# A new written order for the first three head pairs and the steady loop of an attention and soft-MoE kernel, with 66-column values and three more resident weight tiles

## The chip, the core and the metric

The kernel runs on one core of a Trainium2 chip. The metric is the device time of one execution in microseconds (us); one run of the changed kernel is compared with runs of the kernel before on the same chip. The engines are TensorE (PE in the rows; PEld is its weight load), VectorE (DVE), ScalarE (ACT), GpSimd (POOL) and SyncE (SP), which issues most DMAs.

## The reference

Attention over 8 batches of 8 heads, 576 positions of 64 numbers, and a soft mixture of experts on its output, all in float32:

```python
q_rot, k_rot = rotate(q), rotate(k)
scores = (1 / sqrt(D)) * q_rot @ k_rot.T
attn = exp(scores - scores.max(-1)); attn /= attn.sum(-1) + 1e-09
x = (attn @ v) -> (4608, 512)              # 8 heads side by side
logits = x @ phi                           # 32 slots, 4 for each of 8 experts
d = softmax of logits over all 4608 rows;  slot_input = d.T @ x
slot_out[e] = relu(slot_input[e] @ w1[e]) @ w2[e]      # w1 512x1024, w2 1024x512
out = softmax of logits over the 32 slots @ slot_out
```

## The kernel before

The 64 heads are worked as 32 pairs of heads; four pairs make a batch. For each pair p the work is cut into named steps, each a small function that issues its instructions on its engines:

- load0, load1 (line 136, SP): rotary inputs of q and k into one of two x buffers, 576 KB each; load_v (161): the values with a column of ones.
- spin0, spin1 (141, GpSimd): four multiplications each with cosines and sines; "rotations" below. join (146, VectorE) adds the halves. high0, high1 (150, ScalarE) cast to float16 into an operand buffer; low (155, VectorE) takes the remainder, after which the x buffer is free for pair p+2.
- m00 to m31 and m_rem (171, 181): a coarse score product on PE and a maximum over it on VectorE; m_min, m_turn, m_half (193 to 206) turn the maxima into a row, m_rows (208) sends that row by two small DMAs into the tile peak, from SP (for pair 0 from ScalarE's queue).
- t0 to t7 (214): one score part each, eight float16 matmuls, the last two of them with the peaks; ScalarE follows with the exponential. t8 (229) is the remainder part of the 64 last positions.
- av0 to av4 (249): the products with the values. One of av0 to av3 is 18 units; a float32 unit is two matmul instructions, so 36 stand in the trace. Units run two side by side on halves of the array (four in av4). The ones column gives the row sums.
- o_out (278, ScalarE) copies the result out of PSUM, recip (289, VectorE) inverts the sums, norm (295, GpSimd) multiplies into the x tile xn of the batch, natural and natural_out (321, 327) transpose it on PE.
- Once per batch: logits (336) and bs0 to bs6, which run the statistics, the slot product (382: transposes, then matmuls that read xn) and the combine weights.

The score, maximum, transpose and remainder steps share three PSUM buffers of two banks (168); each product waits until the reader of the buffer three before it is done. The value products have one buffer.

The order of all this is written by hand as numbers: WHEN gives each step a due time for a pair (line 51; one pair is 4 units), EARLY (62) replaces it for named steps of the first pairs, and lines 609 to 618 sort the steps by these and issue them. Within one engine instructions run in the order issued; the times themselves are not enforced. Ahead of that, pair 0 is loaded and rotated in halves on VectorE (588 to 602).

Weights are 64 tiles of 512 KB (32 of w1, 32 of w2). N_W tiles of the pool wp are loaded along the pairs, one per pair from pair 2 on (556); N_CST and N_WA tiles follow when the x buffers are done (481), one and N_WE when the operand buffers are done (492), N_WL when the attention's tiles are done (501). The other tiles are loaded in the last stage (714 to 717 and 808), where the slots run through the experts (725 to 759), and the result is combined and sent out in 18 DMAs of 512 KB (772).

Of the kernel before, what the change touches and what calls it, by code (L numbers as in the profile page):

```python
# [19 lines left out]
DM = H * D  # L20
# [7 lines left out]
N_W = 24  # L28
N_WA = 5
N_WB = 2  # L30
N_WE = 3
# [17 lines left out]
CUT = 320  # L49
WIDE = True  # L50
WHEN = {
    "load0": -13.475, "spin0": -13.456, "load1": -13.036, "spin1": -12.384, "join": -11.941, "high0": -11.78,
    "high1": -11.78, "low": -8.673, "m21": -8.574, "m20": -8.467, "m30": -7.842, "m10": -7.783, "m11": -7.689,
    "m_rem": -6.685, "m00": -5.636, "m01": -5.354, "m31": -4.383, "m_min": -2.621, "weights": -1.922, "m_turn":
# [3 lines left out]
    5.267, "recip": 7.247, "norm": 8.094, "natural": 10.815, "natural_out": 10.826, "logits_late": 10.828,  # L58
    "logits_out_late": 11.426, "logits": 13.466, "logits_out": 14.024, "bs0": 14.124, "bs1": 15.06, "bs2":
    17.43, "bs3": 19.118, "bs4": 19.678, "bs5": 20.487, "bs6": 22.6,  # L60
}
EARLY = {
# [3 lines left out]
    -16.25, ("m_rem", 0): -16, ("m_min", 0): -15.75, ("m_turn", 0): -15.5, ("m_half", 0): -15.25, ("m_rows", 0):  # L66
    -15, ("heat", 0): -14.75, ("join0", 1): -14.5, ("high0", 1): -14.25, ("m00", 1): -14, ("m01", 1): -13.75,
    ("m10", 1): -13.5, ("m11", 1): -13.25, ("low", 1): -13, ("load0", 3): -12.75, ("load1", 3): -12.5, ("spin0",
    2): -12.25, ("spin1", 2): -12,
}  # L70
QL, QH, KH, KL = range(4)
TERMS = ((KH, QH), (KH, QL), (KL, QH), (None, None))


# [818 lines left out]
```

## Time and profile before

| | us |
|---|---|
| median of 3 runs | 553.19 |
| lowest and highest | 552.36, 553.56 |
| the profiled execution's own time | 553.2 |
| its span from the first to the last instruction | 551.3 |

A row of the page's slices cuts the span into 40 equal parts of 13.8 us; a digit is the busy share in tenths, and PEclk is the granted clock of TensorE in tenths of full speed. The chain of waits follows the work that ended last back to the start; each of its rows is a stretch of that chain. A group of lines gives count, busy time, mean duration and idle time before.

### The profile page before, as it was taken

What the parts mean: (1) busy time and instruction counts of PE and PEld (TensorE: products, weight loads), DVE (VectorE), ACT (ScalarE), POOL (GpSimd) and SP (SyncE); (2) the same over time, 40 slices, a digit from 0 to 9 for tenths busy, and PEclk for the clock granted to TensorE, in tenths of its full rate; (3) what the DMA queues carried; (4) which work ended last, traced back from release to release, by engine and by line L of the source; (5) the groups of instructions that cost most, each with busy time, mean ns of one, the idle gap of its engine ahead of it and who ended that gap; (6) DMA issues with size and microseconds to landing.
All of it is one profiled execution on the core that took longest, in us unless ns stands there. A gap on an engine that the chain in (4) does not pass through costs nothing.

```text
span 551.3 us, 23417 instructions
## 1 busy us (share of the span) xinstructions
PE 510.1 (93%) x10420; PEld 376.9 (68%) x10420; DVE 366.0 (66%) x610; ACT 313.2 (57%) x688; POOL 283.3 (51%) x356
## 2 busy tenths in 40 slices
PE   3658999999999999999999999999999999899982
PEld 2226777778778777877777778677877777644551
DVE  5777877886787778777877787678777611232352
ACT  2124666666666656675666666666666566254441
POOL 2954666666576557655965686558662211210000
PEclk9657999999999999999999999999999999999997
DMA  7242644444444444444444444443330532549998
GB/s 243 92 172 66 210 157 167 156 151 152 151 152 150 152 152 150 152 151 152 151 152 150 150 153 153 150 150 113 113 113 27 217 104 65 204 144 410 409 416 340
DMA packets 28484, 93.87 MB, mean 170 GB/s; under 512 B 4064, under 2 KB 5856, under 8 KB 28384
## 3 DMA queue, kind: packets, MB, share of 16 engines
q1 hardware_dynamic: 28370, 92.37, 47.0%
q8 instruction: 82, 1.34, 1.0%
q14 instruction: 18, 0.15, 0.1%
q10 hardware_dynamic: 14, 0.00, 0.0%
HBM read 82.85 MB, written 9.44 MB: 167 GB/s over the span
## 4 chain that ended last, share of the span: by engine, by line
PE 84%; DVE 5%; DMA 5%; POOL 1%; ACT 1%; issue 1%; SPq 0%; ACTq 0%; DVEq 0%; POOLq 0%
PE o_ps L255 31%; PE s_ps L226 23%; PE s_ps L177 7%; PE s_ps L325 4%; PE s_ps L240 3%; PE s_ps L729 3%; PE s_ps L342 2%; DVE nm L179 2%; DMA w_exp<-in_w 2%; PE s_ps L185 2%; DMA x_in<-in_qk 2%; PE s_ps L201 1%; PE s_ps L396 1%; POOL x_in L144 1%; PE s_ps L753 1%; DMA out<-w_exp 1%
## 5 line engine op out<-in xcount | busy, mean ns | idle before, releaser
L144 POOL TENSOR_TENSOR x_in<-x_in,cs_sb 128x288 f32<-128x288 f32 x248 | 198.1, 833 | 103.0 <-DMA x_in<-in_qk 90.0
L179 DVE TENSOR_REDUCE nm<-s_ps 128x2 f32<-128x576 f32 x256 | 184.6, 754 | 76.9 <-PE s_ps L177 75.2
L227 ACT ACTIVATE a_t<-s_ps 128x576 f32<-128x576 f32 x256 | 153.5, 653 | 129.6 <-PE s_ps L226 129.4
L255 PE MATMUL o_ps<-v_in,a_t 128*64 128x65 f32 x4608 | 163.0, 225 | 0.7 <-ACT a_t L227 0.7
L255 PEld LDWEIGHTS o_ps<-v_in,a_t 128*64 128x64 f32 x4608 | 145.5, 138 | 26.5 <-issue 21.1
L226 PE MATMUL s_ps<-hl 64*128 64x288 f16 x1536 | 134.0, 286 | 2.9 <-DVE nm L179 2.5
L226 PEld LDWEIGHTS <-hl 64*128 64x128 f16 x1536 | 71.2, 95 | 32.3 <-issue 15.1
L226 PE MATMUL s_ps<-peak,lift 64*128 64x288 f16 x512 | 74.4, 286 | 1.1 <-DMA peak<-mr 1.1
L177 PE MATMUL s_ps<-hl 64*128 64x288 f16 x512 | 65.8, 293 | 9.4 <-DVE nm L179 6.9
L301 POOL TENSOR_TENSOR xn<-o_sb,rr 128x512 f32<-128x512 f32 x31 | 48.3, 1558 | 34.8 <-DVE rr L293 33.4
L153 ACT CAST hl<-x_in 128x576 f16<-128x576 f32 (+1 forms) x66 | 40.9, 678 | 26.8 <-DVE x_in L148 25.0
L148 DVE TENSOR_TENSOR x_in<-x_in 128x1152 f32<-128x1152 f32 (+2 forms) x36 | 46.5, 1291 | 3.3 <-POOL x_in L144 3.2
L157 DVE TENSOR_TENSOR hl<-x_in,hl 128x1152 f16<-128x1152 f32 x32 | 44.9, 1402 | 0.5 <-ACT hl L153 0.5
L177 PEld LDWEIGHTS <-hl 64*128 64x128 f16 x512 | 25.4, 95 | 25.8 <-issue 10.5
L416 POOL TENSOR_TENSOR ln<-ln,cm 128x160 f32<-128x160 f32 x7 | 9.4, 1348 | 46.7 <-DVE cm L415 46.7
L226 PEld LDWEIGHTS <-lift 64*128 64x128 f16 x512 | 25.7, 95 | 7.7 <-issue 1.3
L187 DVE TENSOR_REDUCE nm<-s_ps 128x2 f32<-128x576 f32 x32 | 24.3, 759 | 5.2 <-PE s_ps L185 5.0
L255 PEld LDWEIGHTS o_ps<-v_in,a_tr 64*64 64x64 f32 x1152 | 21.5, 134 | 7.5 <-issue 7.4
L255 PE MATMUL o_ps<-v_in,a_tr 64*64 64x65 f32 x1152 | 26.0, 224 | 0.0
L325 PE MATMUL s_ps<-id_sb,xn 128*128 128x128 f32 x160 | 23.7, 279 | 1.7 <-DVE xn L316 1.7
L240 PE MATMUL s_ps<-hl 64*64 64x320 f16 (+1 forms) x384 | 22.9, 291 | 0.6 <-issue 0.6
L325 PEld LDWEIGHTS s_ps<-id_sb,xn 128*128 128x128 f32 x160 | 16.9, 140 | 9.4 <-issue 8.6
(175 smaller groups left out, 490.6 us busy)
## 6 DMA issues: line engine op xcount, KB each, us to landing
x_in<-in_qk SPq DMA_DIRECT2D x62, 576.0 KB
w_exp<-in_w SPq DMA_DIRECT2D x63, 512.0 KB
v_in<-in_v SPq DMA_DIRECT2D x32, 325.0 KB
out<-w_exp SPq DMA_DIRECT2D x18, 512.0 KB
x_in<-in_qk SPq DMA_DIRECT2D x4, 288.0 KB
cs_sb<-in_cs SPq DMA_DIRECT2D x2, 288.0 KB
wk<-in_w SPq DMA_DIRECT2D x1, 512.0 KB
peak<-mr SPq DMA_DIRECT2D x31, 2.0 KB
```

The source lines that it names most:

```text
L144: eng.tensor_tensor(out=x[:, :, c], in0=x[:, :, c], in1=cs_sb[:, :, c], op=ALU.mult)
L148: nc.vector.tensor_tensor(out=x[:, t, 0, c], in0=x[:, t, 0, c], in1=x[:, t, 1, c], op=ALU.add)
L153: nc.scalar.copy(out=halves[p][:, 1 + t, c], in_=loaded[p][:, t, 0, c])
L157: nc.vector.tensor_tensor(out=hl[:, 0:4:3], in0=x[:, :, 0], in1=hl[:, 1:3], op=ALU.subtract)
L177: nc.tensor.matmul(s[c, h, 0:HC], lhsT=hl[rows[h], QH, P * j + c.start:P * j + c.stop], rhs=hl[rows[h], KH, half[n]], start=True, stop=True)
L179: nc.vector.tensor_reduce(out=nms[p][:, n, j:8:4], in_=s[:, :, 0:HC], axis=AX.X, op=ALU.max, negate=True)
L226: nc.tensor.matmul(s[c, h, 0:HC], lhsT=lhs, rhs=rhs, start=(x == 0), stop=(x == 3))
L227: nc.scalar.activation(out=ats[p, b][:, :, half[n]], in_=s[:, :, 0:HC], func=AF.Exp, scale=SCALE)
L240: nc.tensor.matmul(s[rows[h ^ n], n, 0:w] if n else s[rows[h], 0, 512 - w:512], lhsT=lhs, rhs=rhs, start=(x == 0), stop=(x == 3))
L255: nc.tensor.matmul(o[rows[c], h, 65 * u:65 * u + 65], lhsT=lhs, rhs=v, start=(i == 0 and u == first), stop=stop)
L301: eng.tensor_tensor(out=xn[:, :, 0:4], in0=t[:, :, 0:4, 0:64], in1=rr[:, :, 0:4].unsqueeze(3).broadcast_to([P, 2, 4, 64]), op=ALU.mult)
L325: nc.tensor.transpose(t[:, P * j:P * j + P], xns[b][:, j, pp * P:pp * P + P], id_sb)
```

## The change

The order numbers are new, both for the steady loop and, for every step of pairs 0, 1 and 2, for the start. N_W goes from 24 to 28 and N_WE from 3 to 2. There is one xn tile instead of two and there are three operand buffers instead of four. The values have two columns of ones, so that a unit of the value product has 66 columns and its rows lie 66 numbers apart in PSUM and in the copies. The listing of EARLY is cut.

```diff
--- before.py
+++ after.py
@@ -25,10 +25,10 @@
 CM = 4096.0
 BIG = 3.0e38
 HC = S // 2
-N_W = 24
+N_W = 28
 N_WA = 5
 N_WB = 2
-N_WE = 3
+N_WE = 2
 N_WL = 1
 N_X = 5
 N_O = 2
@@ -47,26 +47,47 @@
 N_A = 3
 N_AR = 1
 CUT = 320
+VW = 66
+N_HL = 3
+N_XN = 1
 WIDE = True
 WHEN = {
-    "load0": -13.475, "spin0": -13.456, "load1": -13.036, "spin1": -12.384, "join": -11.941, "high0": -11.78,
-    "high1": -11.78, "low": -8.673, "m21": -8.574, "m20": -8.467, "m30": -7.842, "m10": -7.783, "m11": -7.689,
-    "m_rem": -6.685, "m00": -5.636, "m01": -5.354, "m31": -4.383, "m_min": -2.621, "weights": -1.922, "m_turn":
-    -1.57, "m_half": -1.488, "m_rows": -0.172, "t0": 0, "t5": 0.097, "t1": 0.15, "t6": 0.268, "trickle0": 0.55,
-    "t8": 1.396, "trickle1": 1.55, "t4": 2.038, "load_v": 2.313, "av0": 2.403, "trickle2": 2.55, "t7": 2.782,
-    "t3": 2.79, "av2": 3.319, "trickle3": 3.55, "av3": 3.997, "t2": 4.028, "av1": 4.176, "av4": 4.327, "o_out":
-    5.267, "recip": 7.247, "norm": 8.094, "natural": 10.815, "natural_out": 10.826, "logits_late": 10.828,
-    "logits_out_late": 11.426, "logits": 13.466, "logits_out": 14.024, "bs0": 14.124, "bs1": 15.06, "bs2":
-    17.43, "bs3": 19.118, "bs4": 19.678, "bs5": 20.487, "bs6": 22.6,
+    "load0": -9.5660, "load1": -9.2923, "spin0": -9.2495, "spin1": -9.1951, "join": -8.6148, "high1": -8.5102,
+    "high0": -7.7527, "low": -5.7077, "m01": -4.7860, "m21": -4.6203, "m10": -4.0010, "m11": -3.9990, "m31":
+    -3.8399, "m30": -3.6599, "m00": -3.6538, "m20": -3.6507, "m_rem": -3.2198, "m_min": -1.9015, "m_turn":
+    -1.2741, "m_half": -1.2400, "weights": -1.0103, "load_v": -0.9825, "m_rows": -0.3931, "t0": 0.0000, "t7":
+    0.1234, "t1": 0.3483, "trickle0": 0.5500, "trickle1": 1.5500, "t8": 1.6955, "trickle2": 2.5500, "av0":
+    2.7124, "t2": 3.2150, "t6": 3.2160, "t5": 3.3121, "t3": 3.3621, "t4": 3.3631, "trickle3": 3.5500, "av3":
+    3.8550, "av1": 4.0015, "av2": 4.3433, "av4": 4.3578, "o_out": 5.2000, "recip": 11.3621, "norm": 12.5850,
+    "natural": 14.5258, "natural_out": 14.6310, "logits_late": 14.6330, "logits": 14.9987, "logits_out":
+    15.0778, "logits_out_late": 15.2310, "bs0": 15.3754, "bs1": 16.0452, "bs2": 16.3082, "bs3": 18.6955, "bs4":
+    18.8882, "bs5": 20.0488, "bs6": 23.2242,
 }
 EARLY = {
...
+    ("low", 0): -10015.2, ("m21", 0): -10012.6, ("m10", 0): -10010.6, ("m_rem", 0): -19.7239, ("m01", 0):
+    -19.7229, ("m30", 0): -19.2249, ("spin0", 1): -17.3334, ("m00", 0): -11.1708, ("m20", 0): -9.6275, ("m11",
+    0): -9.3361, ("m31", 0): -8.3516, ("spin1", 1): -7.6792, ("m_min", 0): -7.4843, ("join0", 1): -7.4833,
+    ("load0", 2): -3.7748, ("m_turn", 0): -3.6049, ("heat", 0): -3.3212, ("m_half", 0): -3.2702, ("join1", 1):
+    -2.2295, ("high1", 1): -2.0637, ("high0", 1): -1.575, ("load1", 2): -1.2863, ("low", 1): -1.0997, ("m11",
+    1): -1.088, ("m_rows", 0): -0.7274, ("m01", 1): -0.5995, ("t8", 0): -0.2355, ("t0", 0): -0.1016, ("m21", 1):
+    0.2211, ("t1", 0): 0.329, ("m10", 1): 0.3399, ("m30", 1): 0.6838, ("t2", 0): 0.6899, ("spin0", 2): 0.6977,
+    ("spin1", 2): 0.8581, ("join", 2): 0.8727, ("load_v", 1): 0.9223, ("t4", 0): 0.9233, ("t3", 0): 1.0977,
+    ("m00", 1): 1.1147, ("high1", 2): 1.1367, ("m_rem", 1): 1.1429, ("high0", 2): 1.1587, ("av0", 0): 1.4005,
+    ("m20", 1): 1.9295, ("t7", 0): 1.9305, ("m31", 1): 2.1643, ("m_min", 1): 2.1821, ("av1", 0): 2.237,
+    ("m_turn", 1): 2.257, ("m_half", 1): 2.2755, ("low", 2): 2.4753, ("t6", 0): 3.0355, ("m11", 2): 3.0722,
+    ("t5", 0): 3.1918, ("m31", 2): 3.2158, ("m_rows", 1): 3.2339, ("m01", 2): 3.2793, ("av3", 0): 3.3978,
+    ("m30", 2): 3.4347, ("t1", 1): 3.4357, ("m20", 2): 3.7798, ("av2", 0): 3.922, ("m00", 2): 4.1088, ("t0", 1):
...
 }
 QL, QH, KH, KL = range(4)
 TERMS = ((KH, QH), (KH, QL), (KL, QH), (None, None))
@@ -87,7 +108,7 @@
     trans = ctx.enter_context(ExitStack())
     att = trans.enter_context(tc.tile_pool(name="att", bufs=1))
     early = ctx.enter_context(ExitStack())
-    stk = early.enter_context(tc.tile_pool(name="stk", bufs=4))
+    stk = early.enter_context(tc.tile_pool(name="stk", bufs=N_HL))
     right = ctx.enter_context(ExitStack())
     io = right.enter_context(tc.tile_pool(name="io", bufs=1, side="right"))
     banks = ctx.enter_context(ExitStack())
@@ -159,7 +180,7 @@
     vts = {}
 
     def load_v(p):
-        vts[p] = att.tile([P, 2 * NB + 2, 65], F32, name="v_in", bufs=2)
+        vts[p] = att.tile([P, 2 * NB + 2, VW], F32, name="v_in", bufs=2)
         nc.sync.dma_start(out=vts[p], in_=v[p])
 
     nms = {}
@@ -252,7 +273,7 @@
         o, vt, at = os_[p], vts[p], ats.pop((p, i))
 
         def unit(lhs, c, h, u, v, stop=False):
-            nc.tensor.matmul(o[rows[c], h, 65 * u:65 * u + 65], lhsT=lhs, rhs=v, start=(i == 0 and u == first), stop=stop)
+            nc.tensor.matmul(o[rows[c], h, VW * u:VW * u + VW], lhsT=lhs, rhs=v, start=(i == 0 and u == first), stop=stop)
 
         if i < NB:
             first = 0
@@ -270,17 +291,17 @@
 
     xts = {}
     xns = {}
-    xn_sb = [xp.tile([P, 5, DM], F32, name=f"xn{i}") for i in range(2)]
+    xn_sb = [xp.tile([P, 5, DM], F32, name=f"xn{i}") for i in range(N_XN)]
     for t in xn_sb:
         nc.gpsimd.memset(t[64:P, 4], 0.0)
     osb = {}
 
     def o_out(p):
-        osb[p] = t = att.tile([P, 2, 5, 65], F32, name="o_sb", bufs=N_O)
+        osb[p] = t = att.tile([P, 2, 5, VW], F32, name="o_sb", bufs=N_O)
         o = os_.pop(p)
-        nc.scalar.copy(out=t.rearrange("p h u x -> p h (u x)")[:, :, 0:260], in_=o[:, :, 0:260])
+        nc.scalar.copy(out=t.rearrange("p h u x -> p h (u x)")[:, :, 0:4 * VW], in_=o[:, :, 0:4 * VW])
         for h in range(2):
-            nc.scalar.copy(out=t[0:64, h, 4], in_=o[rows[h], h, 260:325])
+            nc.scalar.copy(out=t[0:64, h, 4], in_=o[rows[h], h, 4 * VW:5 * VW])
 
     rrs = [const.tile([P, 2, 5], F32, name=f"rr{i}") for i in range(2)]
     for t in rrs:
@@ -295,7 +316,7 @@
     def norm(p, eng):
         b, pp = divmod(p, NP)
         if pp == 0:
-            xns[b] = xn_sb[b % 2]
+            xns[b] = xn_sb[b % N_XN]
         xn = xns[b][:, :, pp * P:(pp + 1) * P].rearrange("p j (h x) -> p h j x", h=2)
         t, rr = osb.pop(p), rrs[p % 2]
         eng.tensor_tensor(out=xn[:, :, 0:4], in0=t[:, :, 0:4, 0:64],
@@ -304,9 +325,9 @@
                           in1=rr[0:64, :, 4].unsqueeze(2).broadcast_to([64, 2, 64]), op=ALU.mult)
 
     def norm_last(p):
-        o = os_.pop(p)[:, :, 0:325].rearrange("p h (u x) -> p h u x", x=65)
+        o = os_.pop(p)[:, :, 0:5 * VW].rearrange("p h (u x) -> p h u x", x=VW)
         rr, pp = rrs[p % 2], p % NP
-        odd = small.tile([P, 2, 65], F32, name="odd", bufs=1)
+        odd = small.tile([P, 2, VW], F32, name="odd", bufs=1)
         for h in range(2):
             nc.scalar.copy(out=odd[0:64, h], in_=o[rows[h], h, 4])
         nc.vector.tensor_scalar_add(out=rr[:, :, 0:4], in0=o[:, :, 0:4, 64], scalar1=1e-9)
@@ -856,7 +877,7 @@
     vm = vr[:, :, :128 * NB].reshape(NPAIR, 2, NB, 128, D).transpose(0, 3, 2, 1, 4).reshape(NPAIR, 128, 2 * NB, D)
     ve = np.stack([vr[:, :, 128 * NB:], vr[:, ::-1, 128 * NB:]], axis=3).reshape(NPAIR, 128, 2, D)
     vl = np.concatenate([vm, ve], axis=2)
-    vl = np.concatenate([vl, np.ones_like(vl[..., :1])], axis=-1)
+    vl = np.concatenate([vl, np.ones_like(vl[..., :VW - D])], axis=-1)
 
     w1 = moe_w1.reshape(2, 4, 2, 2, 128, 2, 512).transpose(0, 5, 2, 1, 4, 3, 6).reshape(4 * E, 128, 1024)
     w2 = moe_w2.reshape(2, 4, 2, 4, 128, 2, 256).transpose(5, 0, 2, 1, 4, 3, 6).reshape(4 * E, 128, 1024)
```

What the numbers make of one period of the steady loop on PE, with the pair relative to p in brackets (none stands for p), without the pieces that come once per batch:

```text
before: t0 t2(-1) t5 t1 m30(+2) | av1(-1) | m10(+2) t6 m11(+2) | av4(-1) m_rem(+2) t8 | t4 m00(+2) |
        av0 m_turn(+1) | m01(+2) t7 t3 | natural(-2) | av2 | m21(+3) m20(+3) m31(+2) | av3
after:  m10(+1) t0 m11(+1) | av1(-1) | t7 m31(+1) m30(+1) | av2(-1) | m00(+1) t1 m20(+1) |
        av4(-1) m_rem(+1) t8 | natural(-3) | av0 m_turn(+1) | m01(+2) t2 t6 t5 t3 t4 m21(+2) | av3
```

In the same way the start, after the prologue, the first column the pair:

```text
before: PE 0: m00 m01 m10 m11 m20 m21 m30 m31 m_rem m_turn heat, 1: m00 m01 m10 m11 m21 m20 m30 m_rem,
        2: m21 m20, 1: m31, 0: t0 t5 t1, 2: m30 m10, 0: t6, 2: m11 m_rem, 0: t8 t4, 2: m00, 0: av0, ...
        0: av2 av3 av1 av4; VectorE has join1(1) after m21(0), ScalarE m_rows(0) ahead of high0(1)
after:  PE 0: m21 m10 m_rem m01 m30 m00 m20 m11 m31 m_turn heat, 1: m11 m01, 0: t8 t0, 1: m21, 0: t1,
        1: m10 m30, 0: t2 t4 t3, 1: m00 m_rem, 0: av0, 1: m20, 0: t7, 1: m31, 0: av1, 1: m_turn, 0: t6,
        2: m11, 0: t5, 2: m31 m01, 0: av3, 2: m30, 1: t1, 2: m20, 0: av2, 2: m00, 1: t0, 2: m10, 0: av4;
        VectorE has join0(1) join1(1) after m_min(0), ScalarE high1(1) high0(1) ahead of m_rows(0)
```

## Rows read from the trace of the kernel before

**Rows 1.** The page: its first line, and of its part 2 PE, clock and traffic in 40 slices.
```profile
span 551.3 us, 23417 instructions
...
PE   3658999999999999999999999999999999899982
...
PEclk9657999999999999999999999999999999999997
...
GB/s 243 92 172 66 210 157 167 156 151 152 151 152 150 152 152 150 152 151 152 151 152 150 150 153 153 150 150 113 113 113 27 217 104 65 204 144 410 409 416 340
```

**Rows 2.** Stage windows, start to 45 us: stretch, length, busy time (instructions) by engine.
```profile
15.00:30.00 15.00, 8.37 (x45) 3.94 (x43) 11.23 (x16) 1.61 (x3) 11.21 (x14) 0.61 0.22 74
30.00:45.00 15.00, 7.85 (x66) 4.85 (x67) 11.70 (x14) 4.99 (x8) 11.66 (x13) 0.50 0.46 158
```

**Rows 3.** Chain of waits, 12 to 49 us: start, duration (us), what.
```profile
13.30 3.21 DVE nm L179 x5
...
20.55 0.18 DVE min L195
...
28.11 1.36 DVE hl L157
...
29.48 3.73 DMA x_in<-in_qk
...
33.34 5.82 POOL x_in L144 x7
```

**Rows 4.** Timeline of PE, 0 to 70 us: start, duration (us), instructions merged.
```profile
46.87 2.17 PE L255 MATMUL o_ps<-v_in,a_t 128*64 128x65 f32 x36
...
58.12 0.23 PE L255 MATMUL o_ps<-v_in,a_tr 64*64 64x65 f32 x2
```

**Rows 5.** Timelines of VectorE and ScalarE, 0 to 70 us.
```profile
17.20 1.10 DVE L148 TENSOR_TENSOR x_in<-x_in 128x576 f32<-128x576 f32 x1
...
18.34 0.67 ACT L153 CAST hl<-x_in 128x576 f16<-128x576 f32 x1 [6.43 <-DVE x_in L148]
...
21.74 1.13 ACTq L210 DMA_DIRECT2D peak<-mr  x1
22.89 0.52 ACTq L211 DMA_DIRECT2D peak<-mr  x1
```

**Rows 6.** Chain of waits on the plateau, 200 to 226 us.
```profile
212.39 0.47 PE s_ps L177 x6
212.86 1.20 PE o_ps L255 x36
214.06 2.07 PE s_ps L226 x32
...
217.73 0.49 PE s_ps L226 x8
...
218.34 0.68 PE o_ps L255 x34
```

**Rows 7.** Chain of waits at the end, 440 us to the end.
```profile
451.13 1.46 PE s_ps L342 x64
...
456.62 2.25 PE o_ps L255 x72
...
517.58 10.37 DMA w_exp<-in_w
```

**Rows 8.** Groups by line and form, whole span: count, busy us, mean ns, idle before.
```profile
L144 POOL TENSOR_TENSOR x_in<-x_in,cs_sb 128x288 f32<-128x288 f32 x248 | 198.1, 833 | 103.0 <-DMA x_in<-in_qk 90.0 <-DMA id_sb<-in_ident 9.5 <-DVE x_in L148 3.0
L179 DVE TENSOR_REDUCE nm<-s_ps 128x2 f32<-128x576 f32 x256 | 184.6, 754 | 76.9 <-PE s_ps L177 75.2
L255 PE MATMUL o_ps<-v_in,a_t 128*64 128x65 f32 x4608 | 163.0, 225 | 0.7 <-ACT a_t L227 0.7
...
L301 POOL TENSOR_TENSOR xn<-o_sb,rr 128x512 f32<-128x512 f32 x31 | 48.3, 1558 | 34.8 <-DVE rr L293 33.4 <-ACT xt L334 0.8 <-ACT a_t L227 0.6
...
L255 PE MATMUL o_ps<-v_in,a_tr 64*64 64x65 f32 x1152 | 26.0, 224 | 0.0
```

More of the change, by code (lines that the diff above doesn't have):

```diff
@@ L49 @@
 CUT = 320
+VW = 66
+N_HL = 3
+N_XN = 1
 WIDE = True
 WHEN = {
-    "load0": -13.475, "spin0": -13.456, "load1": -13.036, "spin1": -12.384, "join": -11.941, "high0": -11.78,
-    "high1": -11.78, "low": -8.673, "m21": -8.574, "m20": -8.467, "m30": -7.842, "m10": -7.783, "m11": -7.689,
-    "m_rem": -6.685, "m00": -5.636, "m01": -5.354, "m31": -4.383, "m_min": -2.621, "weights": -1.922, "m_turn":
[3 rows of a table removed]
-    5.267, "recip": 7.247, "norm": 8.094, "natural": 10.815, "natural_out": 10.826, "logits_late": 10.828,
-    "logits_out_late": 11.426, "logits": 13.466, "logits_out": 14.024, "bs0": 14.124, "bs1": 15.06, "bs2":
-    17.43, "bs3": 19.118, "bs4": 19.678, "bs5": 20.487, "bs6": 22.6,
[3 rows of a table added]
+    -1.2741, "m_half": -1.2400, "weights": -1.0103, "load_v": -0.9825, "m_rows": -0.3931, "t0": 0.0000, "t7":
[3 rows of a table added]
+    "natural": 14.5258, "natural_out": 14.6310, "logits_late": 14.6330, "logits": 14.9987, "logits_out":
+    15.0778, "logits_out_late": 15.2310, "bs0": 15.3754, "bs1": 16.0452, "bs2": 16.3082, "bs3": 18.6955, "bs4":
+    18.8882, "bs5": 20.0488, "bs6": 23.2242,
 }
 EARLY = {
[3 rows of a table removed]
[L66 to L69, printed above, removed]
[3 rows of a table added]
+    ("load0", 2): -3.7748, ("m_turn", 0): -3.6049, ("heat", 0): -3.3212, ("m_half", 0): -3.2702, ("join1", 1):
[6 rows of a table added]
+    ("m_turn", 1): 2.257, ("m_half", 1): 2.2755, ("low", 2): 2.4753, ("t6", 0): 3.0355, ("m11", 2): 3.0722,
[4 rows of a table added]
+    ("av0", 1): 6.9412, ("m_min", 2): 7.0216, ("m_turn", 2): 7.1357, ("m_half", 2): 7.2769, ("m_rows", 2):
[5 rows of a table added]
+    ("recip", 1): 13.5847, ("natural", 0): 13.7449, ("natural_out", 0): 14.1101, ("recip", 2): 15.215, ("norm",
+    2): 15.6059, ("norm", 1): 16.8154, ("natural", 1): 17.9791, ("natural_out", 1): 18.0735, ("natural", 2):
+    21.6965, ("natural_out", 2): 22.3948, ("small_loads", 0): 23.215,
 }
```

10 rows, old and new, of the table EARLY are left out of this document.

## The prediction

> **What bounds the kernel now.** I read the page first, then the stage windows, then the chain of waits, and last the timelines of single engines where the chain points. The page says that TensorE is busy nearly everywhere, but it also shows three stages with different limits: the first three slices, where PE stands at 3 to 6 tenths and its clock is granted at half for much of the time; a long plateau at 9; and the last slices, where PE is still "busy" but the memory traffic jumps from about 150 to over 400 GB/s [rows 1]. The windows confirm the first: in 15 to 45 us PE does 45 and 66 instructions per 15 us, while VectorE and GpSimd are busy for nearly 12 of the 15 [rows 2].
>
> The start is an order problem. The chain runs low(0), the row maxima of pair 0, the minimum, then the maxima of pair 1, low(1) at 28.11, the load of pair 3 at 29.48 (its buffer is free only after low(1)), and eight rotations of pair 3 on GpSimd from 33.34 [rows 3]. Only after that does the first value product of pair 0 start, at 46.87, and at half clock: 2.17 us where it later takes 1.20 [rows 4, 6]. Yet the operands of pair 0 were complete at 13.3 and its row maxima at 20.7 [rows 3]; nothing but the written order holds its scores back. On the plateau the chain is PE alone. Its blocks have fixed prices: a score part 0.49, a maximum part 0.12, a value product 1.20, and a group of three maxima between two value products 0.47, not 0.36 [rows 6]: entering this kind of matmul after another costs 0.11. Two value products side by side take 2.25, so the second costs 1.05 and entering costs 0.15 [rows 7]. At the end PE waits 10.37 us for a weight tile [rows 7], with the DMA at about 410 GB/s through the last four slices [rows 1]: this stage is paid by the byte.
>
> **Part by part. The start.** Up to low(0) at 13.30 nothing changes. Then nine maximum reductions follow without the half join of pair 1 (1.10, rows 5) between them, so the minimum ends at about 20.73 - 1.0 = 19.7 [rows 3]. The two half joins of pair 1 follow: 21.9. ScalarE has high1, high0 of pair 1 (0.67 each) and then issues the row peaks of pair 0 (1.13 + 0.52): 23.2 and 24.9 [rows 5]. This is a move for the worse: before, the peaks were issued at 21.74, ahead of the second cast. ScalarE has nothing else queued behind it but the first exponential, which needs the peaks anyway. How long the 2 KB take to land no row tells; between nothing and the 3.73 us of a 576 KB load [rows 3] I take 2, so the last term of the first score part runs at 27. From there PE has, up to the end of av4(0), in the new order: ten score parts (4.9), thirteen maxima (1.6), four value products (4.8), av4 (0.68), remainder and transpose (about 0.5), and six entries (0.7): 13.2 us at full clock [rows 6, 7]. VectorE over the same stretch, from low(1) at 24.6: sixteen reductions at some 0.70, two joins of 1.4, one low of 1.36, 15.6 us [rows 8, 3]; it ends level with PE, so the two will wait for each other now and then. PE comes out of a nearly idle stretch and, as in 28 to 48 us before, starts at half clock: I add 2.5 for that and the waits together. av4(0) ends at 43; before it ended at 58.35 [rows 4]. At that point the old order had done more: two score parts and seven or eight maxima ahead, 1.9 us of PE time. Gain 58.35 - 43 - 1.9 = **13.4, taken as 13**. Bounds: 10 if half clock holds through most of the 13.2 us, 15 if neither clock nor waits cost anything. The loads and rotations cover it: pair 3 is loaded when low(1) ends (24.6 instead of 29.48), its eight rotations end some 10.5 us later as before (33.34 + 8 x 0.83 - 29.48), at 35, and its join stands behind the maxima of pair 2, at 37. The value load of pair 1 now stands ahead of the peaks of pair 1 on SP and waits for nothing; the small loads go far behind, where their first user is still later.
>
> **The steady order.** Old: five groups of score and maximum parts per pair, four value products (none adjacent), one remainder group, one transpose group. New: four such groups, the rest the same. One entry less, -0.11 per pair [rows 6]. The batch pieces move the other way: the two transposes of the batch statistics and the slot product now split score groups, two entries per four pairs, +0.05 per pair. Five score parts now stand in a row where there were four; four cost 2.07 where 4 x 0.49 + 0.11 would be 2.07 [rows 6], so the three banks hide ScalarE; a fifth may add 0.05. Over some 28 pairs: **-2 taken**, between -4 (old irregular stalls go as well) and +5 (the tighter order adds 0.2 per pair).
>
> **One x buffer, three operand buffers.** The single x buffer makes the first normalisation of a batch wait for the slot product of the batch before. Behind it on GpSimd stand eight rotations (6.7) and behind those the join; per pair GpSimd has 6.7 + 2.1 = 8.8 us of work in 12.6 [rows 8], and the rotations are wanted only at the end of the period, by my count 0.6 us after they end in that period and 5 us after they end in the other three. Cost nothing; if that cover is gone, VectorE's join and ScalarE's cast come late and each microsecond of it costs up to 7 in all, once per batch. The operand buffer of pair p is asked for by the cast of pair p+3 right behind the exponential of the last score part of pair p, on the same engine: nothing to wait for.
>
> **66 columns.** A value product is 36 instructions in 18 passes of two; there are 4608 / 2 + 1152 / 4 = 2592 passes [rows 8]. A pass takes 1.05 / 18 = 58.3 ns for 65 columns, 54.2 at two clock cycles per column, so 4.1 over. The logits do 16 passes of 128 and 64 columns in 1.46 [rows 7]; 1.28 is two cycles per column, 0.15 the entry, which leaves about 2 ns over per pass. If 65 pays for being odd, 66 costs 55.0 + 2 = 57: -1.3 ns a pass, -3.4 us. If not, it costs 0.83 more: +2.2. The nearest row with an even width is the logits', of the same type; its rounding makes the gain uncertain by half, so I take 1 ns: **-2.5**. The copies and the normalisation grow by under 2% and lie beside PE.
>
> **More weights resident.** Of 64 tiles, 24 + 2 + 5 + 1 + 3 + 1 = 36 were on chip before the last stage, now 28 + 2 + 5 + 1 + 2 + 1 = 39. Three tiles of 0.524 MB less at 0.41 MB per us: **-3.8**. The four loads that move into the plateau find its DMA half idle [rows 1]. Bounds: -3.8, and 0 if PE were the limit; it waits 10.37 for a tile [rows 7], so it is not.
>
> **Sum.** Against the profiled run, 551.3 of span plus 1.9 around it = 553.2, which is the median too: 553.2 - 13 - 2 - 2.5 - 3.8 = **532**.
>
> **Rivals.** *Width costs.* The extra column is paid at the plain rate: +2.2 for -2.5, so 536.6. For it: the moving rows start at odd offsets for one head and even for the other, and I see no slower head. Against: the logits' smaller overhead. The Trainium skill, page "TensorE: Matmul & The Clock Gate", section "Back-to-back issue gap", gives a gap that grows with the columns at the clock rate and knows no odd widths; by that rule this rival is what happens, and no run so far shows an even width in this place. *The start is only half won.* VectorE and half clock stretch the first pair, gain 6: 539. For it: the reductions take as long as PE's work there; against: neither is longer than it. *The weights bring nothing*, because the freed time waits for the output instead: 535.8; against it the DMA is full in the last four slices. *Slower.* The join stands at the end of a period directly ahead of the next cast on ScalarE, and the next exponentials behind that; if the rotations are late, ScalarE stalls each pair. The 19.3 us of the other terms are lost from 0.63 us per pair on (30.6 pairs); at 1 us the time is 534 + 31 = 565. Against it: the rotations end some 5 us before the join in ordinary periods.
>
> **How the numbers follow.** Forecast 0.62 (527 to 535), width 0.16, start half won 0.10, weights 0.05, slower 0.05, nothing gained on balance 0.02. The measurement can tell about 0.2%, 1.1 us, from no change. Faster 0.93, same 0.02, slower 0.05. The range takes in the first four cases without their outer ends: 526 to 542.
>
> **What would show it.** av0(0) near 33 and av4(0) near 43; PE at 9 from the second or third slice; periods of 12.6 with four score groups; two adjacent value products still 2.1 or less for 66 columns; the wait for a weight tile still about 10, with the DMA full for 3.8 us less. Wrong would be: GpSimd's normalisation ending later than the eight rotations allow, a wait of PE on VectorE in each period, or value products above 1.20.

## The result and the profile after

The changed kernel takes **536.47 us** (median of 4 runs, 535.86 to 537.46), the kernel before beside it 553.38 (552.36 to 554.58): ratio 0.9695, 95% interval 0.9671 to 0.972. The gain is 16.9 us where I had added up 21.3. The profiled execution is the 536.47 one, with a span of 534.4, so the two spans differ by the same 16.9.

The lines of the page that answer to [rows 1]:

```profile
span 534.4 us, 23424 instructions
PE   4799999999999999999999999999999999899992
PEclk9699999999999999999999999999999999999997
GB/s 251 121 159 181 184 155 155 163 156 153 160 155 157 155 155 160 155 120 165 176 141 87 167 173 165 93 157 169 181 111 155 42 252 42 172 171 404 408 393 319
```

PE stands at 9 from the third slice on, and the clock with it. The windows of [rows 2] (stretch, length, busy time of PE, PEld, DVE, ACT, POOL, clock, DMA share, GB/s) show the same; PE does 99 and 327 instructions where it did 45 and 66:

```profile
15.00:30.00 15.00, 11.80 (x99) 6.43 (x98) 13.00 (x18) 4.45 (x9) 12.51 (x15) 0.66 0.49 178
30.00:45.00 15.00, 14.52 (x327) 11.34 (x325) 14.21 (x19) 9.61 (x20) 12.22 (x13) 1.00 0.32 117
```

The timeline of PE, for [rows 4]: the first value product of pair 0 at 30.61, at full speed, and the last matmul of its last one from 40.90 on.

```profile
30.61 1.27 PE L276 MATMUL o_ps<-v_in,a_t 128*64 128x66 f32 x36
...
40.90 0.22 PE L276 MATMUL o_ps<-v_in,a_tr 64*64 64x66 f32 x1
```

The chain on the plateau, for [rows 6]: five score parts in a row, and a value product that still takes 1.20 with 66 columns.

```profile
205.72 2.50 PE s_ps L247 x40
208.22 0.18 PE s_ps L198 x2
208.40 1.20 PE o_ps L276 x36
```

To see where the gain comes from and where it goes again, I took from the timelines the start of the last matmul of the last value product of a pair (58.1 for pair 0 before [rows 4], 40.9 after), and the start of the last stage's first matmul:

| us | pair 0 | pair 5 | pair 25 | pair 31 | last stage begins | span |
|---|---|---|---|---|---|---|
| before | 58.1 | 122.8 | 395.6 | 474.5 | 489.1 | 551.3 |
| after | 40.9 | 105.7 | 379.9 | 459.7 | 474.5 | 534.4 |
| ahead by | 17.2 | 17.1 | 15.7 | 14.8 | 14.6 | 16.9 |

So the start won 17.2 at this mark, the steady stretch lost 2.6 of it (I had expected it to win 2.6: 4.5 less the 1.9 of work done ahead), and the last stage won 2.3. From one mark to the next an ordinary pair takes 12.68 instead of 12.73. The two pairs at the end of a batch take 15.96 + 13.15 instead of 14.4 + 14.3.

**The batch.** The chain in the second of those periods (start, duration, what) goes through VectorE, whose join takes 1.90 us there and 1.35 in ordinary periods:

```profile
237.36 0.61 issue
237.97 1.90 DVE x_in L169
239.88 0.68 DVE nm L200
```

GpSimd's timeline shows what runs beside it. The norm of the next batch's first pair stands 11.28 us at the head of the queue, until the slot product (L417) has read the one x tile; eight spins stand behind it, and behind those the norm of the second pair, which so falls on the join. Its large half runs from 237.62, and the join that starts at 237.97 is long; its small half takes 1.51 us where the first pair's takes 0.40:

```profile
228.39 1.05 POOL L322 TENSOR_TENSOR xn<-o_sb,rr 128x512 f32<-128x512 f32 x1 [11.28 <-PE s_ps L417]
229.40 0.40 POOL L324 TENSOR_TENSOR xn<-o_sb,rr 64x128 f32<-64x128 f32 x1
...
230.05 7.20 POOL L165 TENSOR_TENSOR x_in<-x_in,cs_sb 128x288 f32<-128x288 f32 x8
...
237.62 1.04 POOL L322 TENSOR_TENSOR xn<-o_sb,rr 128x512 f32<-128x512 f32 x1
238.62 1.51 POOL L324 TENSOR_TENSOR xn<-o_sb,rr 64x128 f32<-64x128 f32 x1
```

The two engines hold each other up. The Trainium skill, page "SBUF — State Buffer", section "SBUF: two separate sides", has a pair of ports that VectorE and GpSimd share, held for a whole instruction while the other waits; the trace agrees, with 0.55 us more for the join and 1.1 for the norm. (Before I saw the join's length, I took it to be late, and the expectations of experiments 9 and 11 say so; it starts right behind the maximum ahead of it, there and in the ninth and twelfth kernels.)

**Near the end of the plateau** the chain has 4.70 us for the peaks of pair 30, of which TensorE is idle for 1.04. The waits of SP's queue and its timeline (start, duration of the issue):

```profile
SPq L498 <- DVE hl L178: 10.8, 1, 10.8
```

```profile
424.50 0.33 SPq L498 DMA_DIRECT2D w_exp<-in_w  x1
424.93 0.37 SPq L184 DMA_DIRECT2D v_in<-in_v  x1
425.35 0.42 SPq L498 DMA_DIRECT2D w_exp<-in_w  x1
425.83 0.52 SPq L231 DMA_DIRECT2D peak<-mr  x1
```

A weight tile that takes the place of the last x buffer waits 10.8 us there for the last pair's low; values and peaks stand behind it, and the peaks then land behind two tiles. The kernel before had a stall of 1.1 us on its peaks too, so this is no loss of the change, but it can be had.

**The last stage** took 62.2 us before and takes 59.9. The chain no longer waits for a weight tile where it waited 10.37 [rows 7]; from 500 to 524 us it is PE with copies between, and the DMA moves 414 and 383 GB/s beside it. Its windows, columns as above:

```profile
504.50:514.50 10.00, 10.00 (x122) 5.70 (x122) 6.14 (x10) 5.11 (x10) 0.00 (x0) 1.00 1.03 414
514.50:524.50 10.00, 8.62 (x55) 6.50 (x55) 6.66 (x11) 6.51 (x12) 0.00 (x0) 1.00 0.96 383
```

### The profile page after: what moved, and what is told of

Same layout as the page of the kernel before. It is cut to its first block, busy times and chain, and to the rows that moved or that the text cites. A ratio compares the mean times of both kernels' runs of the same rounds, so it can differ in the third digit from the quotient of the medians.

```text
span 534.4 us, 23424 instructions
## 1 busy us (share of the span) xinstructions
PE 505.3 (95%) x10420; PEld 381.5 (71%) x10420; DVE 370.1 (69%) x610; ACT 312.8 (59%) x688; POOL 273.3 (51%) x355
## 4 chain that ended last, share of the span: by engine, by line
PE 83%; DVE 7%; DMA 3%; ACT 2%; issue 2%; POOL 1%; SPq 1%; DVEq 0%; ACTq 0%; POOLq 0%
PE o_ps L276 29%; PE s_ps L247 22%; PE s_ps L198 7%; PE s_ps L346 4%; PE s_ps L261 4%; DVE x_in L169 3%; PE s_ps L750 3%; PE s_ps L363 2%; DMA x_in<-in_qk 2%; DVE nm L200 2%; PE t_ps L801 2%; PE o_ps L774 1%; PE s_ps L774 1%; PE s_ps L222 1%; POOL x_in L165 1%
## 5 line engine op out<-in xcount | busy, mean ns | idle before, releaser
L165 POOL TENSOR_TENSOR x_in<-x_in,cs_sb 128x288 f32<-128x288 f32 x248 | 207.5, 874 | 54.0 <-DMA x_in<-in_qk 38.5
L276 PE MATMUL o_ps<-v_in,a_t 128*64 128x66 f32 x4608 | 162.7, 224 | 0.0
L247 PE MATMUL s_ps<-hl 64*128 64x288 f16 x1536 | 133.2, 283 | 2.5 <-issue 0.7
L247 PEld LDWEIGHTS <-hl 64*128 64x128 f16 x1536 | 76.3, 94 | 20.5 <-issue 4.9
L322 POOL TENSOR_TENSOR xn<-o_sb,rr 128x512 f32<-128x512 f32 x31 | 32.4, 1046 | 114.3 <-PE s_ps L417 87.6
L198 PE MATMUL s_ps<-hl 64*128 64x288 f16 x512 | 71.6, 291 | 1.6 <-DVE nm L200 1.2
L178 DVE TENSOR_TENSOR hl<-x_in,hl 128x1152 f16<-128x1152 f32 x32 | 53.7, 1678 | 1.8 <-ACT hl L174 1.8
L169 DVE TENSOR_TENSOR x_in<-x_in 128x1152 f32<-128x1152 f32 (+2 forms) x36 | 50.1, 1393 | 0.3 <-POOL x_in L165 0.2
L198 PEld LDWEIGHTS <-hl 64*128 64x128 f16 x512 | 28.3, 93 | 23.8 <-issue 9.3
L276 PE MATMUL o_ps<-v_in,a_tr 64*64 64x66 f32 x1152 | 26.9, 224 | 0.4 <-issue 0.3
L226 ACT ACTIVATE mr<-s_ps 9x128 f16<-9x128 f32 x32 | 8.5, 267 | 26.4 <-PE s_ps L222 26.3
L302 ACT COPY o_sb<-o_ps 128x528 f32<-128x528 f32 x31 | 18.6, 600 | 8.9 <-PE o_ps L276 8.6
```

The source lines that it names most:

```text
L165: eng.tensor_tensor(out=x[:, :, c], in0=x[:, :, c], in1=cs_sb[:, :, c], op=ALU.mult)
L169: nc.vector.tensor_tensor(out=x[:, t, 0, c], in0=x[:, t, 0, c], in1=x[:, t, 1, c], op=ALU.add)
L178: nc.vector.tensor_tensor(out=hl[:, 0:4:3], in0=x[:, :, 0], in1=hl[:, 1:3], op=ALU.subtract)
L198: nc.tensor.matmul(s[c, h, 0:HC], lhsT=hl[rows[h], QH, P * j + c.start:P * j + c.stop], rhs=hl[rows[h], KH, half[n]], start=True, stop=True)
L247: nc.tensor.matmul(s[c, h, 0:HC], lhsT=lhs, rhs=rhs, start=(x == 0), stop=(x == 3))
L276: nc.tensor.matmul(o[rows[c], h, VW * u:VW * u + VW], lhsT=lhs, rhs=v, start=(i == 0 and u == first), stop=stop)
```

## The experiments

Medians of before were 553.29 (first four kernels), 552.74 (next three), 553.05 (next three) and 553.53 (last two); ratios are to these.

**1. The old start in the changed kernel.**
```
 EARLY = { ... }        # the 33 entries of the kernel before; everything else as changed
```


> The changed kernel with the old numbers for the start, everything else new. If the start is the main source (av4 of pair 0 ends at 41 instead of 58 us in the changed kernel, less some 2 us of work that stood done in the old order), this run loses 13 to 16 us against the changed kernel: 550 to 552, and av4 of pair 0 ends at 56 or later. Rival, that the gain comes from the steady order or the tail: below 545.

Measured: 542.52 us (541.54 to 543.62), ratio 0.9794 [0.9751, 0.9837]. A miss: only 6 us are lost. On PE's timeline the first product of pair 0 starts at 36.44 and the last matmul of its last one at 47.85, ten us ahead of before although the first entries are the old ones:

```profile
36.44 1.69 PE L259 MATMUL o_ps<-v_in,a_t 128*64 128x66 f32 x36
...
47.85 0.23 PE L259 MATMUL o_ps<-v_in,a_tr 64*64 64x66 f32 x2
```

So the larger part of the start comes from the table of the steady numbers. There the join stands 11.94 quarter periods ahead of its pair's first score before, 8.61 after, and the maxima 8.57 to 4.38 before, 4.79 to 3.22 after. With the old numbers seven of the nine maxima of pair 2, and the spins, the join and the casts of pair 3, are issued ahead of pair 0's first value product; with the new ones they stand behind it. The join and casts of pair 2 stand ahead of it in both. The join's difference, 3.33 quarters of 12.7 us, is 10.6 us; the mark moved by 10.2 (58.1 to 47.9). That the two numbers agree is no proof yet; experiments 7 and 8 put the lead to the test.

**2. 65 columns again.**
```
-VW = 66
+VW = 65
```


> The changed kernel with 65 columns again. My forecast of 2.5 us gained by the even width says 538 to 540. The lone value products of the changed kernel still show 1.20 us at 66 columns, so by that row the width is worth nothing: 535 to 537. Plain price per column (0.83 ns a pass): 534.3.

Measured: 536.72 us (535.0 to 538.44), ratio 0.9693 [0.9661, 0.9725]. The ordinary period is 12.67 us against 12.68. The groups by form, 66 columns and 65 (count, busy us, mean ns):

```profile
L276 PE MATMUL o_ps<-v_in,a_t 128*64 128x66 f32 x4608 | 162.7, 224 | 0.0
```

```profile
L276 PE MATMUL o_ps<-v_in,a_t 128*64 128x65 f32 x4608 | 162.1, 224 | 0.0
```

Neither a gain nor a cost: 0.01 us per pair is 0.3 us over 31 pairs.

**3. Three fewer weight tiles resident; 4. the same with two x tiles.**
```
-N_W = 28  /  N_WE = 2          # 3 and 4
+N_W = 24  /  N_WE = 3
-N_XN = 1                       # 4 alone
+N_XN = 2
```


> The changed kernel with 24 tiles along the pairs and three behind the operand buffers, as before, so three tiles more in the last stage. Paid by the byte: 3.8 us more, 540.3. If PE's own order limits the last stage of the changed kernel, as its chain suggests (no wait for a tile left in it), the last stage was 2.3 shorter than before and the loss is about that: 538 to 539.

> The run before with two x tiles, so that no normalisation waits for the slot product of the batch before. The theory that the single x tile costs the 0.5 us that a join comes late in one period of each batch: 3 us less than with one x tile. Rival, that the batch pieces themselves cost it by splitting groups of score parts: no difference.

Measured: 538.89 us (536.93 to 541.56), 0.9734 [0.9696, 0.9772], and 537.82 (536.27 to 538.7), 0.9711 [0.9681, 0.9741]. The last stage takes 63.2 us in both, against 59.9 in the changed kernel, and its chain waits for weights again:

```profile
495.30 10.16 DMA w_exp<-in_w
...
505.52 10.13 DMA w_exp<-in_w
```

The three tiles are worth 3.3 us in the traces and 2.4 in the medians, not 3.8. (The kernel before had as many tiles on chip as these two, and 62.2; the 1.0 us between them is not explained.) Two x tiles shorten the second batch period from 13.14 to 12.90, as the norm no longer waits for the slot product (GpSimd's timeline of the fourth kernel; the spins follow at 222.84 instead of 229.93 in the third, and the second pair's norm is done at 237.3, ahead of the join, which takes 1.35):

```profile
220.90 1.05 POOL L322 TENSOR_TENSOR xn<-o_sb,rr 128x512 f32<-128x512 f32 x1 [4.09 <-ACT a_t L248]
...
222.84 7.20 POOL L165 TENSOR_TENSOR x_in<-x_in,cs_sb 128x288 f32<-128x288 f32 x8 [0.37 <-DMA x_in<-in_qk]
```

That is 0.24 us for each of 6 batches, 1.4 us, and in the first batch as much in a later period (12.92, now 12.68). The medians say 1.1, with overlapping ranges. It is not all gain: in two of the batches the spins, which now start early, meet the join of the first period instead (1.91 us at 223.0 and 277.6), and that period takes 16.34 and 16.35 for 15.96.

**5. Peaks of the last pair by ScalarE's queue.**
```
-m_rows(p, nc.sync if p else nc.scalar)
+m_rows(p, nc.sync if 0 < p < NPAIR - 1 else nc.scalar)
```


> The changed kernel, with the transfer of the last pair's maxima (m_rows, four small pieces) issued by ScalarE's queue instead of SyncE's, where in the changed kernel it stands behind two weight tiles of 512 KB and a tile of values and the chain of waits shows 4.70 us for it at 425.83. If those loads ahead of it in SyncE's queue are what makes it late: the period that holds the stall falls from 14.8 us to about 12.7, nothing of it comes back in the drain, and the time is 533.5 to 534.5 us, 2 to 3 under the changed kernel. If TensorE's idle time there is due to something else that ends at the same place (the late join, the search for the maxima), the piece in the chain only changes its name and the time stays within 0.7 us of 536.5. If ScalarE pays for the issue (0.5 to 1.1 us between its casts) at this place, the gain is under 1.5 us.

Measured: 536.53 us (535.26 to 539.18), 0.9696 [0.9649, 0.9743]. It decides nothing: the stall belongs to pair 30, whose peaks still went by SP, and there it is again, 5.02 us in the chain.

**6. Four score parts in a row.**
```
-"high1": -8.5102   "t4": 3.3631
+"high1": -8.0050   "t4": 3.9900
```


> The changed kernel, with the last of its five scores that stand in a row moved behind the second product with the values (and the cast that goes with it later in ScalarE's order), so that only four scores follow one another. In the changed kernel five in a row take 2541 ns where five single ones take 5 x 490. If the fifth waits for a bank that the score two before it still holds: 0.09 us less per pair, the plain period falls from 12.68 to about 12.6 and the time to about 534 to 534.7 us. The rival is that a switch between the two tilings of the array costs as much as the wait (one more entry in the order, 0.1 us per pair): then the period stays at 12.68 or rises to 12.78, and the time is 536.5 to 539.5 us.

Measured: 539.49 us (539.4 to 540.9), 0.9763 [0.9724, 0.9803]. The rival was right, and its price too low: the ordinary period is 12.94. In the chain the moved score part costs the entry (0.61 for 0.49), and then TensorE's maxima wait for ScalarE, 0.13 us in each ordinary pair; the two make up the 0.26:

```profile
206.57 2.01 PE s_ps L247 x32
...
209.91 0.61 PE s_ps L247 x8
...
210.54 0.66 ACT a_t L248
```

**7. The shorter lead in the kernel before, pairs 2 and 3; 8. for all pairs.**
```
+("join", 2): -0.6148, ... ("m_min", 3): 10.0985     # 7: EARLY, 28 entries: the changed numbers + 4p
-"load0": -13.475, ... "m_half": -1.488              # 8: WHEN, these 20 steps
+"load0": -9.566, ... "m_half": -1.24
```


> The kernel before, with its own start, values, tiles and steady order, except that pairs 2 and 3 take the changed kernel's numbers for the join, the casts, and the search for the maxima, so that this work no longer stands ahead of pair 0's scores on VectorE and GpSimd. The changed kernel with the old order of its first pairs was 542.5 us, only 6 slower than with the new one, so some 10 us of the gain come from something else than that order. If it is the shorter lead of the maxima in the steady numbers: the last product of pair 0 ends near 48 us instead of 58.1, and the time is 543 to 546 us. If it is another part of the change (the single x tile, the three operand buffers, the steady order of TensorE): the last product of pair 0 stays at 56 us or later, and the time is 550 us or more. Between them lies the case that the work left out at the start is only put off and comes back within the first batch: pair 0 early, pair 5 as before (122.8 us), time 549 to 553.

> The kernel before, with its own start, values, tiles and steady order of scores and products, except that the loads, spins, join, casts and the search for the maxima of every pair take the changed kernel's numbers (in the run before this was so for pairs 2 and 3 alone; pair 0 ended at 47.9 us, as in the changed kernel with the old start, but the old numbers of pair 4 and later stood against them and pair 1 ended at 71.7). If the shorter lead of that work is what the changed kernel with the old start gained: pair 0 ends near 48, pair 5 near 111 to 113 instead of 122.8, and the time is 542.5 to 546 us. If the old steady order can't do with the shorter lead (maxima late in each pair), pair 0 ends near 48 but the plain period is over 12.9, and the time is 549 us or more. If the lead has nothing to do with it, pair 5 ends at 120 or later.

Measured: 558.18 us (557.09 to 559.72), 1.0096 [1.0066, 1.0125], and 649.22 (647.33 to 650.17), 1.1723 [1.169, 1.1757]. Both are slower than the kernel before, but in both pair 0 is early (marks at 47.9 and 49.7), as the lead theory has it. In the seventh the spins of pair 3 still stand ahead of pair 0's first product, so they are not what held it up: what moved behind it are the maxima of pair 2 and the join and casts of pair 3. There the work of pairs 4 and later, with the old numbers, is met at once: pair 1 ends at 71.7, pair 5 at 126.6. In the eighth the old order of TensorE cannot do with the short lead: ordinary periods are 15.23 us, and PE waits for VectorE's maxima in each pair. The waits of PE from 60 to 470 us (total, times, longest):

```profile
PE s_ps L274 <- DVE nm L227: 40.3, 24, 4.7
PE s_ps L233 <- DVE nm L227: 14.6, 24, 0.6
PE s_ps L288 <- DVE nm L227: 5.5, 24, 0.2
```

In the changed kernel the first of these rows reads 0.7, once. So the short lead needs the new steady order: the order is what lets the maxima come late without TensorE waiting, and the lead's worth is paid out once, at the start. The new order with the old lead was not run.

**9. The first norm of a batch behind the spins.**
```
+("norm", 4k): 16k + 14.81, ("natural", 4k): 16k + 14.815, ("natural_out", 4k): 16k + 14.816   # k = 1..6
```


> The changed kernel, with the norm of the first pair of batches 1 to 6 moved behind the next eight spins in GpSimd's order (and its transposes and their cast just behind it). In the changed kernel that norm waits 11.28 us for the slot product of the batch before, which still reads the one x tile; the spins behind it have had their data for some 5 us, the join that follows is late (0.61 + 1.90 us in the chain) and the second period of the batch takes 13.15 us instead of 12.90 as with two x tiles. If the wait at the head of GpSimd's queue makes the late join: the second period falls to 12.9 and the one after the next to 12.68, about 0.25 to 0.5 us for each of 6 batches, 533.5 to 535 us. If the join is late because GpSimd has too much to do there in any order (13.20 of 13.2 us busy), or the transposes now wait for the norm, the periods stay at 13.15 or grow and the time is 536.5 us or more.

Measured: 538.38 us (537.92 to 540.44), 0.9733 [0.9703, 0.9763]. The join takes 1.35 in the second period of all six batches, but the two periods are 15.97 + 13.59, or 16.62 + 12.99: the copy of the product's output on ScalarE waits for the norm, which frees its buffer, and the next product waits for the copy. The chain:

```profile
225.54 4.58 POOL x_in L183 x6
230.12 1.00 POOL xn L340
...
231.51 0.60 ACT o_sb L320
```

**10. Two weight tiles behind the peaks of pair 30.**
```
+("trickle2", 29): 119.61, ("trickle3", 29): 119.62      # m_rows of pair 30 is at 119.607
```


> The changed kernel, with the two weight tiles that stand ahead of the peaks of pair 30 in SyncE's queue moved behind them (pair 30, not the last one: the stall that the earlier run of the peaks on ScalarE's queue left as it was, 5.02 us in the chain). SyncE stands from 413.6 to 424.4 us at the first of these tiles, which waits for the low parts of the last pair, with the values and the peaks behind it; the peaks then land behind 1.35 MB. If that is what makes the peaks late: TensorE's idle time of 1.04 us ahead of the first score of pair 30 goes, the period of 13.9 us falls to 12.9, and the time is 535.2 to 535.8 us. If it comes back at the end, since those weight tiles are 2.5 us later and the stream of weights behind them too, the period falls but the time stays at 536.5. If the peaks are late for another reason, both stay.

Measured: 535.92 us (534.94 to 536.49), 0.9684 [0.9656, 0.9713]. The peaks are issued first (SP's timeline), PE has no wait left between 400 and 450 us, and that period is 13.08 instead of 13.9. The last stage stays at 59.9.

```profile
424.05 0.52 SPq L233 DMA_DIRECT2D peak<-mr  x1
...
425.25 2.52 SPq L500 DMA_DIRECT2D w_exp<-in_w  x5
```

**11. The norm between the two halves of the spins; 12. with experiment 10's edit as well.**
```
+("norm", 4k): 16k + 14.78, ("natural", 4k): 16k + 14.785, ("natural_out", 4k): 16k + 14.786   # k = 1..6
```


> The changed kernel, with the norm of the first pair of batches 1 to 6 between the two halves of the next pair's spins in GpSimd's order. Behind all eight spins the norm ended near 231.4 us, and the copy of the product's output waited for it, so the first periods grew; but the join was on time. With four spins (3.1 to 3.6 us from 223.5) ahead of it the norm can still start at the end of the slot product (228.4 us), the copy has nothing to wait for, and the other four spins end near 233 instead of 237.2. If the queue's order made the late join: first periods of 15.96, second ones of 12.9 instead of 13.15, the one after the next 12.68: 1.5 to 2 us less in 6 batches, 534.5 to 535 us. If the transposes that now stand behind a product and the turn of the maxima cost as much, the second periods stay at 13.15 and the time at 536 to 537 us.

> The changed kernel, with both edits: the norm between the two halves of the spins, and the two weight tiles behind the peaks of pair 30. The second alone brought the period of 13.9 us to 13.08 and the median from 536.5 to 535.9. If both theories hold the gains add up, since they lie in different stretches: 533.8 to 534.6 us. If the norm's place brings nothing: 535.5 to 536.2 us.

Measured: 535.61 us (534.21 to 537.21), 0.9672 [0.964, 0.9703], and **534.29** (533.41 to 536.51), 0.9653 [0.9623, 0.9682]: the fastest version here, though its interval still overlaps that of the changed kernel. In the eleventh the second periods fall to 12.98 in all six batches; five first periods stay at 15.9 to 16.0, and one takes 16.86, with a join of 1.93. In the twelfth all first periods are 15.96, and the second 12.98 in four batches, 13.74 (with a pause of 0.49) and 13.14 in the others. Its trace is of the run that took 536.51, so the gain shows in the periods and not in the span. GpSimd's timeline of the last kernel:

```profile
225.18 3.80 POOL L185 TENSOR_TENSOR x_in<-x_in,cs_sb 128x288 f32<-128x288 f32 x4 [6.38 <-DMA x_in<-in_qk]
229.80 1.05 POOL L342 TENSOR_TENSOR xn<-o_sb,rr 128x512 f32<-128x512 f32 x1 [0.82 <-PE s_ps L437]
...
231.17 3.05 POOL L185 TENSOR_TENSOR x_in<-x_in,cs_sb 128x288 f32<-128x288 f32 x4
```

The first pair's norm starts as early as in the changed kernel, and the second pair's is done (0.39 for its small half) before the join starts at 239.52 and takes 1.35, here and in all six batches:

```profile
238.33 0.39 POOL L344 TENSOR_TENSOR xn<-o_sb,rr 64x128 f32<-64x128 f32 x1
```

```profile
239.52 1.35 DVE L189 TENSOR_TENSOR x_in<-x_in 128x1152 f32<-128x1152 f32 x1
```

So it was the queue's order that put the norm on the join, and a second x tile isn't needed for that.

## Why the prediction was right or wrong

**The sum.** The start won 2.3 us more than I had (15.3 for 13), the steady stretch, where the order, the columns and the x tile work, 5.2 less (0.7 lost, with the 1.9 of work done ahead taken off the 2.6, for 4.5 won), the last stage 1.5 less (2.3 for 3.8): 21.3 + 2.3 - 5.2 - 1.5 is the 16.9 measured. That the total is only 4.4 us off is in part these errors taking each other away.

**The start** won a little more than worked: I had 13 net of the 1.9 us of work done ahead, and 17.2 - 1.9 is 15.3, just past my upper bound. av4(0) ended at 41.1 and not at 43. The step that was too dear is the last term of the first score part at 27: the peaks were read at 25.65 without a wait. From there to the end of av4(0) it took 15.5 us, and 13.2 + 2.5 had said 15.7, but by luck. PE's timeline at that place, and the window of the stretch (columns as above):

```profile
25.65 0.38 PE L261 MATMUL s_ps<-peak,lift 64*64 64x256 f16 x4
```

```profile
25.65:41.12 15.47, 14.59 (x312) 11.04 (x306) 14.71 (x20) 9.54 (x17) 10.20 (x12) 1.00 0.48 169
```

The granted clock was 1.00, its full level, all the way (TensorE had not been idle before, as I had it, but busy for 4.72 of the five us from 20 on), and TensorE was idle for only 0.88. So 2.5 for half clock and waits was 1.6 too much; its work, with the end of the remainder part, took 14.59 where I had counted 13.2. (VectorE's terms beside it add up to 15.4 and not to 15.6; nothing hangs on that.) What I had wrong is where the gain comes from. I costed the order of the first three pairs as the whole cause; taking that order out again, in experiment 1, costs 6 of the 16.9 us, and 7.0 of the 17.2 at pair 0's mark. The other 10.2 come with the shorter lead in the steady numbers, which I never compared, although it can be read off the table. What the new start would bring with the old lead was not run, so this split holds in one order of the two alone.

**The steady order.** The step "-2 taken" counted entries per pair, and for ordinary periods that count was good: -0.11 + 0.05 for the fifth score part, -0.05 measured. (The sum itself slipped: with the 0.05 for the batch pieces the three terms make -0.01 per pair, -0.3 over 28 pairs; the -2 leaves the fifth score part out.) What failed is the batch: I allowed 0.05 per pair, 0.2 per batch, but the two periods at a batch's end take 0.41 more than before (28.70 to 29.11), 0.17 of which goes with the order of experiment 11. And it left out the order's main use, which experiment 8 shows: without it the short lead costs 2.5 us in every pair.

**One x buffer (the tile xn), "cost nothing".** Wrong, by another way than the one I named. I counted the spins' end against the join (0.6 us of slack) and that held: the spins end at 237.25, the join starts behind a maximum at 237.97 in any case. What I left out is the norm of the second pair behind those spins, which then runs beside the join and lengthens it by 0.55 us, 0.24 of the period, in 6 batches. The kernel before has more such collisions: 17 of its 31 large norm halves take 1.97 us or more, each beside a low on VectorE (hence the mean of 1558 ns in [rows 8], 1046 in the changed kernel), and in five batches the small half meets a join there too (1.59 to 1.71 us). But those joins lie in periods of 12.60 to 12.73, where nothing waits for them. So "GpSimd has time" was not enough: it matters when. The three operand buffers showed no wait.

**66 columns, -2.5.** Wrong by all of it; measured 0.0 to 0.3 the other way. The premise that an odd width pays was read from the logits, another tile shape, and fell. The Trainium skill, page "TensorE: Matmul & The Clock Gate", section "Back-to-back issue gap", has a formula for isolated matmuls in which a column costs its clock time, and by it the 66 columns would be 2.2 us slower (the estimate of the rival). Experiment 2 has 0.01 us per pair, so the trace agrees neither with that formula nor with my gain. That the total lies at that rival's 536.6 is chance.

**Weights, -3.8.** The mechanism is right, the size is not: 2.3 in the traces of before and after, 3.3 (2.4 in the medians) in experiment 3. The step that failed is "it waits 10.37 for a tile, so it is not" limited by PE: in the windows around that wait PE was busy for 9.87 and 9.35 of 10 us in the kernel before:

```profile
510.00:520.00 10.00, 9.87 (x140) 5.79 (x136) 1.90 (x4) 3.13 (x8) 0.88 (x1) 1.00 1.02 407
520.00:530.00 10.00, 9.35 (x112) 5.06 (x104) 5.78 (x10) 4.50 (x9) 0.00 (x0) 1.00 1.03 411
```

The wait is one piece of the chain, not idle time of its length, and with three tiles less the chain runs over PE.

## What to carry to other kernels

When a software pipeline's table is re-timed, compare how far ahead of its first use each step stands: the shortening is paid out once, at the start, even where no period gets shorter, and it can be had only with an order that lets those steps come late. In an in-order queue price a wait by everything behind it and by what that work will then run beside: a norm that waits for a single buffer pushed another one onto the join, and reordering half a step brought that back without the second buffer. A long wait in the chain says what came last, not how much time goes when it is taken away; look at how busy the other engine is beside it.

## What the runs showed of the hardware that was not expected

ScalarE's queue issues a transfer while the engine computes. In the changed kernel the first peaks are issued from 22.53 for 1.15 us while two casts of 0.67 run (timeline of ScalarE):

```profile
22.46 0.67 ACT L174 CAST hl<-x_in 128x576 f16<-128x576 f32 x1 [1.49 <-DVE x_in L169]
22.53 1.15 ACTq L231 DMA_DIRECT2D peak<-mr  x1
23.04 0.67 ACT L174 CAST hl<-x_in 128x576 f16<-128x576 f32 x1
```

I had added the two up.

Second, most builds have one to five pauses of TensorE of 0.1 to 1.0 us on the plateau, for which the profile's waits name nothing that was awaited; they move the sums by a microsecond or two. They return at the same instructions: the one before 269.39 us in the changed kernel (0.74 us) stands at the same matmul in six builds. Among the DMA queues on the changed kernel's page is one of the kind instruction (packets, MB, share):

```profile
q8 instruction: 82, 1.34, 1.0%
```

These are transfers of 16 KB, one every 5.5 us or so. Each of the 36 pauses on the plateaus of these kernels ends 2.2 to 2.5 us after the start of such a transfer (the one above after that of 267.0), so by their timing TensorE waits there for its instructions. No run changed these loads.
